# Dense stage of a three-stage kernel: six tiles of 512 tokens in place of eight of 384

## The chip, the cores and the metric

One core of a Trainium2 chip runs the whole program. The metric is device time in microseconds: 999.37 us for the kernel before, the median of three runs (998.09, 999.37 and 1006.32). The engines are TensorE (PE in the rows; its weight loads PEld), VectorE (DVE), ScalarE (ACT), GpSimd (POOL) and SyncE (SP), which only issues transfers here.

## What is computed

Three layers stand one behind the other on 3072 tokens of 512 features, all in fp32:

```python
# 1: attention with a decaying state, per batch (4) and head (8), 768 steps, head size 64
state = gamma * state + outer(k[t], v[t]);  y[t] = scale * (q[t] @ state)
# 2: mixture of experts: 8 experts, the best one by the gate for each token
e = argmax(x @ w_gate + modality_bias[modality_id])
out[mask] = gate_w[mask] * (relu(x[mask] @ w1[e]) @ w2[e])      # 512 -> 1024 -> 512
# 3: dense layer, 512 -> 2048 -> 512
h = x @ w_in
g = h * (1 / (1 + exp(-1.702 * h)))
out = g @ w_out
```

## The kernel before, in words

**Products of fp32 numbers.** Every factor is kept as two fp32r parts, a high one (`h`) and the rest (`l`), and a product is three matmuls: high by high, high by low, low by high. So a step's 4 blocks of 128 features make 12 matmuls in the dense stage's first product.

**Three stages.** Attention runs to about 140 us. From about 115 to 441.8 us the expert stage streams weights: a plan of *slots* (big ones of 256 tokens, B0 to B11, and two tiny ones, T0 and T1, of 32) is worked off by `run_slots`. The tokens of a slot are gathered from DRAM by index (`xg`, L650) and turned on TensorE (L673), the two products are L689 and L707, in tiny slots L738 to L778. The expert rows go to DRAM sorted by slot, with the token's number as one more column (513 columns, `DW`). The dense stage, 441.8 to 991 us, reads these sorted rows back, and scatters its results to the token's place.

**The stream of weights.** A piece is 512 KB, 128x1024. `load` (SyncE's queue, L572) fetches it into a ring of `nraw` = 4 raw buffers. `split` copies the high part on ScalarE (L593, `whi`), takes the rest on VectorE, or for some pieces on GpSimd (L595, `wlo`), and then asks `load` for the next piece: a raw buffer is free when both have read it. The engines work their instructions in program order, so a split that waits for its piece holds up what stands behind it on ScalarE and VectorE; in tiny slots that is the copy `htt` (L771), which the products of L778 read.

**The dense stage.** `T2` = 384 tokens are a tile, so there are 8 tiles of 3 rows (`NR`) of 128 tokens. A tile has 16 steps `f`, one for each 128 of the 2048 hidden features. `d1` does the first product of a step (12 matmuls into `psd`, L1104), the sigmoid on ScalarE (L1107, `sig`), `g` on VectorE (L1109), its high part `gh` on ScalarE (L1114) and the rest `gl` on VectorE (L1115). `d2` does the second product two steps later (`LAG`): for each row three matmuls of 512 columns into `psq` (L1125), one accumulator for each row, a single buffer of each. In the first steps `more_conv` puts the splitting of `w_out` between `g` and `gh`: lines 958 to 983 on ScalarE, VectorE and GpSimd. At the last step of a tile each row's accumulator is copied to `o` (VectorE L1129, ScalarE L1131) and scattered to DRAM by GpSimd (L1133).

**The rows of the next tile.** `yload` fetches a row of 128 tokens into `yg` on SyncE's queue in steps 5, 6 and 7; `turn` in steps 11, 12 and 13 copies the token numbers on GpSimd, turns the row on TensorE (four transposes, L1030) and splits it (ScalarE `yh` L1032, VectorE `yl` L1033). The rows of the first tile are fetched and turned inside the last slot of the expert stage, by a list `tail` of which each unit of work of that slot takes one entry. Behind the expert stage stands a branch (L1079) for slots beyond the plan, which is not taken here; each engine reads the condition and then goes on.

**Buffers.** `gt` (gh, gl) 3, `gg` (sig, g) 2, `yp` (yg) 3, `ot` (o) 3; in PSUM `psd` 3, the turned rows 2, each `psq` 1.

Of the kernel before, what the change touches and what calls it, by code (L numbers as in the profile page):

```python
# [8 lines left out]
F32 = mybir.dt.float32  # L9
# [3 lines left out]
AF = mybir.ActivationFunctionType  # L13
ALU = mybir.AluOpType
AX = mybir.AxisListType
PSUM = bass.MemoryType.PSUM
# [3 lines left out]
N, DM = B * S, H * D  # L20
E, FF = 8, 1024
DFF = 2048
C = 128
# [8 lines left out]
MAXB = 15  # L32
# [3 lines left out]
NB, NT_ = 12, 2  # L36
DW = DM + 1
RP1 = NP1 * BIG
T2 = 384
NF = DFF // C  # L40
AHEAD = 4

# [51 lines left out]
def tile_kernel(ctx, tc, qn, kv, mod, wg, mbias, w1, w2, w_in, w_out, c_qc, c_misc, out):  # L94
    nc = tc.nc
    V = nc.vector
    ctx.enter_context(tc.manual_schedule())
    pool = lambda st, name, bufs, side="left", space=None: st.enter_context(
        tc.tile_pool(name=name, bufs=bufs, side=side, reuse_waits="tile", **({"space": space} if space else {})))
# [10 lines left out]
    ident = M("id")  # L110
# [14 lines left out]
    mm = {}  # L125

    def open_sbuf(st_, nraw, nw):
        for nm, bufs in (("raw", nraw), ("w", nw), ("xg", 1), ("xt", 2), ("h", 3)):
            mm[nm] = pool(st_, "p_" + nm, bufs, "right")
        mm["nraw"], mm["nw"] = nraw, nw  # L130

    mo = ExitStack()
    open_sbuf(mo, 4, 6)


    pa = ExitStack()
# [234 lines left out]
    def T(nm, *sh):  # L371
        if nm not in tb:
            tb[nm] = ct(list(sh), "t_" + nm)
        return tb[nm]

    sc = T("sc", MAXB * E)
# [630 lines left out]

    NR = T2 // C
    NT2 = N // T2
    YG, YT, GT, PO = {}, {}, {}, {}  # L1010
# [1 line left out]
    pad("pad1", "left")  # L1012
    yt = [pool(ctx, "yt0", 1)]

    def yload(t, r, y=None):
        n = t * NR + r
        if y is None:
            y = yp.tile([C, DW], F32, name="yg", tag="yg")
        src, n0 = (ys0, 0) if n < RP1 // C else (ys1, RP1 // C)
        nc.sync.dma_start(y, src[(n - n0) * C:(n - n0 + 1) * C, :])  # L1020
        YG[t, r] = y

    def turn(t, r, ps):
        if r == 0:
            YT[t] = [yt[t % 2].tile([C, 4, T2], F32R, name=f"y{x}", tag=f"y{x}") for x in "hl"]
        y = YG.pop((t, r))
        n = t * NR + r
        nc.gpsimd.tensor_copy(idd[:, n:n + 1], y.bitcast(I32)[:, DM:DW])
        for k in range(4):
            nc.tensor.transpose(ps[:, k, :], y[:, k * C:(k + 1) * C], ident)  # L1030
        yh, yl = (x[:, :, r * C:(r + 1) * C] for x in YT[t])
        nc.scalar.copy(yh, ps)  # L1032
        V.tensor_tensor(out=yl, in0=ps, in1=yh.bitcast(F32), op=ALU.subtract)  # L1033

    def first_loads():
        y = mm["xg"].tile([C, 2, DW], F32, name="yg", tag="xg")
        for r in range(2):
            yload(0, r, y[:, r, :])

    def first_turn(r):  # L1040
        turn(0, r, mm["t"].tile([C, 4, C], F32, name="pyt", tag="pt"))
        if r == 1:
            yload(0, 2, mm["xg"].tile([C, DW], F32, name="yg", tag="xg"))

    cq = []

    def first_conv(stage):
        if stage == 0:
            cq.extend((Conv(NF + NE), Conv(NF + NE + 1)))
        else:  # L1050
            cq[0].A()
            cq[0].B()

    none = lambda: None
    tail = [first_loads, none, none, lambda: first_conv(0), lambda: first_turn(0), lambda: first_turn(1), none, none, lambda: first_turn(2), lambda: first_conv(1)]
    fin = table_final()
    for _ in range(FIN_SLOTS - 1):
        next(fin)
# [15 lines left out]
    mps.close()  # L1074
    mo.close()
    R_ = lambda name, bufs: pool(ctx, name, bufs, "right")
    gt, gg, yp, ot = R_("gt", 3), R_("gg", 2), R_("yp", 3), R_("ot", 3)
    ps_h = pool(ctx, "ps_h2", 3, "left", PSUM)
    with tc.If(tot > 0):  # L1079
        with ExitStack() as xs:  # L1080
# [12 lines left out]
    for f in range(NE, NF):  # L1093
        woh[f] = wo.tile([C, DM], F32R, name=f"woh{f}")
        wol[f] = wo.tile([C, DM], F32R, name=f"wol{f}")
    ps_o, ps_t = (pool(ctx, nm, b, "left", PSUM) for nm, b in (("ps_o2", 1), ("ps_t2", 2)))

    def d1(t, f, mid=None):
        yh, yl = YT[t]
        ps = ps_h.tile([C, T2], F32, name="psd", tag="psd")  # L1100
        m = 0
        for k in range(4):
            for a, b in ((wih, yh), (wih, yl), (wil, yh)):
                nc.tensor.matmul(ps, a[:, k, f * C:(f + 1) * C], b[:, k, :], start=(m == 0), stop=(m == 11), skip_group_check=True)  # L1104
                m += 1
        sig = gg.tile([C, T2], F32, name="sig", tag="sig")
        nc.scalar.activation(sig, ps, AF.Sigmoid, scale=1.702)  # L1107
        g = gg.tile([C, T2], F32, name="g", tag="g")
        V.tensor_tensor(out=g, in0=ps, in1=sig, op=ALU.mult)  # L1109
        if mid:  # L1110
            mid()
        gh = gt.tile([C, T2], F32R, name="gh", tag="gh")
        gl = gt.tile([C, T2], F32R, name="gl", tag="gl")
        nc.scalar.copy(gh, g)  # L1114
        V.tensor_tensor(out=gl, in0=g, in1=gh.bitcast(F32), op=ALU.subtract)  # L1115
        GT[t, f] = (gh, gl)

    def d2(t, fs):
        if fs[0] == 0:
            PO[t] = [ps_o.tile([C, DM], F32, name="psq", tag=f"psq{r}") for r in range(NR)]  # L1120
        for r in range(NR):
            for f in fs:
                gh, gl = GT[t, f]
                for m, (a, b) in enumerate(((gh, woh), (gh, wol), (gl, woh))):
                    nc.tensor.matmul(PO[t][r], a[:, r * C:(r + 1) * C], b[f], start=(f == 0 and m == 0), stop=(f == NF - 1 and m == 2), skip_group_check=True)  # L1125
            if f == NF - 1:
                o = ot.tile([C, DM], F32, name="o", tag="o")
                if r % 2:
                    V.tensor_copy(o, PO[t][r])  # L1129
                else:  # L1130
                    nc.scalar.copy(o, PO[t][r])  # L1131
                n = t * NR + r
                nc.gpsimd.indirect_dma_start(out=outv[n], out_offset=bass.IndirectOffsetOnAxis(ap=idd[:, n:n + 1], axis=0), in_=o, in_offset=None)  # L1133
        for f in fs:
            del GT[t, f]
        if f == NF - 1:
            del PO[t], YT[t]
# [3 lines left out]
    def more_conv(i):  # L1141
        if len(cq) < NF - NE:
            cq.append(Conv(NF + NE + len(cq)))
        at_ = lambda k: cq[k] if 0 <= k < NF - NE else None
        p0, p1, p2 = at_(i + 1), at_(i), at_(i - 1)
        for p, fs in ((p1, "C"), (p0, "A"), (p2, "E"), (p0, "B"), (p2, "F")):
            if p:
                getattr(p, fs)()

    for i, (t, f) in enumerate(seq):  # L1150
        d1(t, f, lambda: more_conv(i) if i <= NF - NE else None)
        if t + 1 < NT2:
            if f in (5, 6, 7):
                yload(t + 1, f - 5)
            elif f in (11, 12, 13):
                turn(t + 1, f - 11, ps_t.tile([C, 4, C], F32, name="pyt", tag="pyt"))
        if LAG <= i < len(seq):
            t, f = seq[i - LAG]
            d2(t, [f])
    d2(NT2 - 1, list(range(NF - LAG, NF)))  # L1160


# [32 lines left out]
```

## Time and profile before

| | us |
|---|---|
| median of three runs | 999.37 |
| the profiled execution | 1003.18 |
| its span, first to last instruction | 1001.5 |
| TensorE busy | 965.8 (96%) |
| VectorE busy | 504.3 (50%) |
| ScalarE busy | 410.3 (41%) |
| GpSimd busy | 177.7 (18%) |
| dense stage, first product L1104 to the last of L1125 | 441.79 to 991.1 |

The mean granted clock of TensorE is 0.988 of full speed. Busy shares are of the whole span and mix the stages; a matmul's record is longer than its share of a stream, since matmuls overlap, so paces are taken from start to start or from a chain of many.

### The profile page before, as it was taken

The numbers are of one execution on the slowest core, as the hardware profiler recorded it, in microseconds if no ns is written. First come the engines' busy times: TensorE is split into PE (matmuls) and PEld (weight loads), VectorE is DVE, ScalarE is ACT, GpSimd is POOL, SyncE is SP. The second block draws the span as 40 slices with busy tenths as digits, with TensorE's granted clock in tenths as the row PEclk, the third lists the DMA queues.
The fourth block names the chain that finished last, engine by engine and source line by source line (L and its number), as shares of the span: only waits on it lengthen the run. The fifth ranks groups of instructions, "written<-read, shape, count | busy, mean of one in ns | idle before, by whom it ended". The sixth has DMA issues, their size and how long they took to land.

```text
span 1001.5 us, 16732 instructions
## 1 busy us (share of the span) xinstructions
PE 965.8 (96%) x6610; PEld 857.7 (86%) x6610; DVE 504.3 (50%) x921; ACT 410.3 (41%) x728; POOL 177.7 (18%) x177
## 2 busy tenths in 40 slices
PE   8999879899999999999999999999999999999995
PEld 7878768799999997778999999999999999999994
DVE  3545559798888876549942322322323223223221
ACT  3423245477767765348742222222322222222221
POOL 2343334223333222003220010010000100100101
PEclk9999989999999999999999999999999999999998
DMA  8777668788788779834410100100001001000000
GB/s 287 222 210 204 113 227 213 251 267 275 285 277 278 262 249 341 304 116 170 136 43 1 32 32 1 32 32 12 26 27 32 32 1 32 32 1 1 32 1 31
DMA packets 43129, 128.18 MB, mean 128 GB/s; under 512 B 6977, under 2 KB 7361, under 8 KB 43041
## 3 DMA queue, kind: packets, MB, share of 16 engines
q1 hardware_dynamic: 34464, 107.96, 34.1%
q0 software_dynamic: 5120, 12.77, 3.6%
q10 hardware_dynamic: 3456, 6.29, 1.8%
q8 instruction: 53, 0.87, 0.4%
q14 instruction: 36, 0.29, 0.1%
HBM read 107.76 MB, written 19.24 MB: 127 GB/s over the span
## 4 chain that ended last, share of the span: by engine, by line
PE 54%; ACT 0%; DVE 0%; POOLq 0%; POOL 0%; issue 0%; ACTq 0%
PE psq L1125 27%; PE psd L1104 26%; PE pyt L1030 1%; ACT L1107 0%; POOLq L1191 0%; DVE ab L963 0%; DVE ab L965 0%; ACT o L1131 0%; ACT ab L958 0%; ACT ab L968 0%; ACT sig L1107 0%; DVE gl L1115 0%; DVE ab L964 0%; POOL out_dram L1133 0%; POOLq L1133 0%
## 5 line engine op out<-in xcount | busy, mean ns | idle before, releaser
L1109 DVE TENSOR_TENSOR g<-psd,sig 128x384 f32<-128x384 f32 x128 | 71.3, 557 | 278.4 <-ACT sig L1107 278.4
L1107 ACT ACTIVATE sig<-psd 128x384 f32<-128x384 f32 x128 | 63.0, 492 | 291.9 <-PE psd L1104 291.9
L1104 PE MATMUL psd<-yh,wih 128*128 128x384 f32 x512 | 172.8, 337 | 0.1
L1104 PE MATMUL psd<-yl,wih 128*128 128x384 f32 x512 | 172.7, 337 | 0.0
L1104 PE MATMUL psd<-yh,wil 128*128 128x384 f32 x512 | 172.6, 337 | 0.0
L1125 PE MATMUL psq<-woh,gh 128*128 128x512 f32 x384 | 153.9, 401 | 0.7 <-ACT gh L1114 0.7
L1125 PE MATMUL psq<-woh,gl 128*128 128x512 f32 x384 | 152.0, 396 | 1.1 <-DVE gl L1115 1.1
L1125 PE MATMUL psq<-wol,gh 128*128 128x512 f32 x384 | 151.7, 395 | 0.0
L595 DVE TENSOR_TENSOR wlo<-raw,whi 128x1024 fp32r<-128x1024 f32 x93 | 113.2, 1222 | 32.7 <-ACT whi L593 28.2
L593 ACT CAST whi<-raw 128x1024 fp32r<-128x1024 f32 x96 | 99.7, 1046 | 39.6 <-issue 17.8
L689 PE MATMUL psh<-xh,whi 128*128 128x256 f32 x384 | 109.7, 286 | 1.1 <-ACT xh L676 1.1
L689 PE MATMUL psh<-xl,whi 128*128 128x256 f32 x384 | 108.2, 282 | 0.1
L689 PE MATMUL psh<-xh,wlo 128*128 128x256 f32 x384 | 108.0, 281 | 0.0
L1133 POOL DMA_INDIRECT out_dram<-o,idd x24 | 23.3, 972 | 461.0 <-DVE o L1129 386.4
L1115 DVE TENSOR_TENSOR gl<-g,gh 128x384 fp32r<-128x384 f32 x128 | 71.5, 559 | 65.0 <-ACT gh L1114 65.0
L1104 PEld LDWEIGHTS psd<-yh,wih 128*128 128x128 f32 x512 | 96.3, 188 | 6.1 <-PEq L1079 0.5
L1104 PEld LDWEIGHTS psd<-yl,wih 128*128 128x128 f32 x512 | 96.3, 188 | 5.5
L1104 PEld LDWEIGHTS psd<-yh,wil 128*128 128x128 f32 x512 | 96.3, 188 | 0.0
L1114 ACT CAST gh<-g 128x384 fp32r<-128x384 f32 x128 | 65.7, 514 | 70.3 <-DVE g L1109 70.2
L1125 PEld LDWEIGHTS psq<-woh,gl 128*128 128x128 f32 x384 | 72.5, 189 | 18.6 <-DVE gl L1115 1.5
L1125 PEld LDWEIGHTS psq<-woh,gh 128*128 128x128 f32 x384 | 72.5, 189 | 12.4 <-ACT gh L1114 1.0
L1125 PEld LDWEIGHTS psq<-wol,gh 128*128 128x128 f32 x384 | 72.7, 189 | 11.5
(195 smaller groups left out, 1516.3 us busy)
## 6 DMA issues: line engine op xcount, KB each, us to landing
raw<-in_w_dram SPq DMA_DIRECT2D x96, 512.0 KB
qk<-in_qn_dram SPq DMA_DIRECT2D x23, 512.0 KB
r<-in_w_in_dram SPq DMA_DIRECT2D x16, 512.0 KB
r<-in_w_out_dram SPq DMA_DIRECT2D x16, 512.0 KB
ys<-yo SPq DMA_DIRECT2D x12, 513.0 KB
yg<-ys SPq DMA_DIRECT2D x24, 256.5 KB
v<-in_kv_dram SPq DMA_DIRECT2D x24, 256.0 KB
xd<-xr ACTq DMA_DIRECT2D x24, 256.0 KB
```

The costliest lines, as they stand in the source:

```text
L593: nc.scalar.copy(hi, raw)
L595: eng.tensor_tensor(out=lo, in0=raw, in1=hi.bitcast(F32), op=ALU.subtract)
L689: nc.tensor.matmul(ps[:, f, :], a[:, k, f * C:(f + 1) * C], b[:, k, :], start=(m == 0), stop=(m == 11), skip_group_check=True)
L1030: nc.tensor.transpose(ps[:, k, :], y[:, k * C:(k + 1) * C], ident)
L1104: nc.tensor.matmul(ps, a[:, k, f * C:(f + 1) * C], b[:, k, :], start=(m == 0), stop=(m == 11), skip_group_check=True)
L1107: nc.scalar.activation(sig, ps, AF.Sigmoid, scale=1.702)
L1109: V.tensor_tensor(out=g, in0=ps, in1=sig, op=ALU.mult)
L1114: nc.scalar.copy(gh, g)
L1115: V.tensor_tensor(out=gl, in0=g, in1=gh.bitcast(F32), op=ALU.subtract)
L1125: nc.tensor.matmul(PO[t][r], a[:, r * C:(r + 1) * C], b[f], start=(f == 0 and m == 0), stop=(f == NF - 1 and m == 2), skip_group_check=True)
L1133: nc.gpsimd.indirect_dma_start(out=outv[n], out_offset=bass.IndirectOffsetOnAxis(ap=idd[:, n:n + 1], axis=0), in_=o, in_offset=None)
```

## The change

The tile of the dense stage is made 512 tokens (6 tiles of 4 rows). To make room, the raw ring of the expert stage goes from 4 to 3 buffers, `yp` and `ot` from 3 to 2, `gg` from 2 to 1, and the turned rows in PSUM from 2 to 1. The sigmoid is written into `g`'s buffer and multiplied in place. The first tile's four rows are fetched on GpSimd's queue in two pairs, the second pair after the second turn, and the `tail` list turns a fourth row. A sigmoid of one column is issued beside the first pair. In the steady tiles rows 0 and 1 are fetched in steps 5 and 6, rows 2 and 3 in steps 11 and 12 behind the turns of rows 0 and 1, and turned in steps 13 and 14. The outputs of the last tile's rows 2 and 3 go through `yp`'s buffers.

```diff
-T2 = 384
+T2 = 512
...
-    open_sbuf(mo, 4, 6)
+    open_sbuf(mo, 3, 6)
...
-    def yload(t, r, y=None):
+    def yload(t, r, y=None, eng=nc.sync):
...
-        nc.sync.dma_start(y, src[(n - n0) * C:(n - n0 + 1) * C, :])
+        eng.dma_start(y, src[(n - n0) * C:(n - n0 + 1) * C, :])
...
-    def first_loads():
+    def first_loads(r0):
         y = mm["xg"].tile([C, 2, DW], F32, name="yg", tag="xg")
         for r in range(2):
-            yload(0, r, y[:, r, :])
+            yload(0, r0 + r, y[:, r, :], nc.gpsimd)
+        if r0 == 0:
+            nc.scalar.activation(T("sc", MAXB * E)[:, 0:1], ident[:, 0:1], AF.Sigmoid)
...
         if r == 1:
-            yload(0, 2, mm["xg"].tile([C, DW], F32, name="yg", tag="xg"))
+            first_loads(2)
...
-    tail = [first_loads, none, none, lambda: first_conv(0), lambda: first_turn(0), lambda: first_turn(1), none, none, lambda: first_turn(2), lambda: first_conv(1)]
+    tail = [lambda: first_loads(0), none, none, lambda: first_conv(0), lambda: first_turn(0), lambda: first_turn(1), none, lambda: first_turn(2), lambda: first_turn(3), lambda: first_conv(1)]
...
-    gt, gg, yp, ot = R_("gt", 3), R_("gg", 2), R_("yp", 3), R_("ot", 3)
+    gt, gg, yp, ot = R_("gt", 3), R_("gg", 1), R_("yp", 2), R_("ot", 2)
...
-    ps_o, ps_t = (pool(ctx, nm, b, "left", PSUM) for nm, b in (("ps_o2", 1), ("ps_t2", 2)))
+    ps_o, ps_t = (pool(ctx, nm, b, "left", PSUM) for nm, b in (("ps_o2", 1), ("ps_t2", 1)))
...
-        sig = gg.tile([C, T2], F32, name="sig", tag="sig")
-        nc.scalar.activation(sig, ps, AF.Sigmoid, scale=1.702)
         g = gg.tile([C, T2], F32, name="g", tag="g")
-        V.tensor_tensor(out=g, in0=ps, in1=sig, op=ALU.mult)
+        nc.scalar.activation(g, ps, AF.Sigmoid, scale=1.702)
+        V.tensor_tensor(out=g, in0=ps, in1=g, op=ALU.mult)
...
-                o = ot.tile([C, DM], F32, name="o", tag="o")
+                last = t == NT2 - 1 and r >= 2
+                o = yp.tile([C, DW], F32, name="yg", tag="yg")[:, 0:DM] if last else ot.tile([C, DM], F32, name="o", tag="o")
...
-            if f in (5, 6, 7):
+            if f in (5, 6):
                 yload(t + 1, f - 5)
-            elif f in (11, 12, 13):
+            if 11 <= f < 11 + NR:
                 turn(t + 1, f - 11, ps_t.tile([C, 4, C], F32, name="pyt", tag="pyt"))
+                if f < 13:
+                    yload(t + 1, f - 9)
```

## Rows read from the trace of the kernel before

**Rows 1.** Page, part 4: the chain that ended last, shares of the span by line.
```profile
PE psq L1125 27%; PE psd L1104 26%; PE pyt L1030 1%; ACT L1107 0%; POOLq L1191 0%; DVE ab L963 0%; DVE ab L965 0%; ACT o L1131 0%; ACT ab L958 0%; ACT ab L968 0%; ACT sig L1107 0%; DVE gl L1115 0%; DVE ab L964 0%; POOL out_dram L1133 0%; POOLq L1133 0%
```
**Rows 2.** Windows: stretch, length, busy of PE, PEld, DVE, ACT, POOL, PEclk, DMA, GB/s.
```profile
441.80:456.20 14.40, 12.60 (x57) 11.17 (x58) 8.04 (x13) 10.32 (x19) 4.07 (x3) 0.88 0.42 142
524.60:934.00 409.40, 409.40 (x2087) 370.67 (x2086) 122.06 (x216) 111.24 (x222) 19.54 (x33) 1.00 0.07 22
450.80:454.20 3.40, 3.39 (x9) 2.71 (x10) 2.79 (x5) 3.09 (x7) 1.29 (x1) 0.53 0.43 154
183.00:186.00 3.00, 0.33 (x1) 0.14 (x1) 2.57 (x11) 1.03 (x1) 0.00 (x0) 1.00 0.86 304
```
**Rows 3.** Chain in order of time: start, us, engine, tile, line, matmuls.
```profile
638.39 2.12 PE psd L1104 x12
640.51 2.10 PE psq L1125 x9
...
655.20 2.08 PE psd L1104 x12
```
**Rows 4.** Timeline, TensorE: start, us, engine, line, operation. Nine matmuls lie between these.
```profile
437.18 0.39 PE L707 MATMUL pso<-whi,hl 128*128 128x512 f32 x1
...
439.22 0.39 PE L707 MATMUL pso<-whi,hl 128*128 128x512 f32 x1
```
**Rows 5.** Timeline, the dense stage's first step; in brackets the idle before and its releaser.
```profile
445.15 1.28 ACT L1107 ACT_TABLE_LOAD   x1 [2.78 <-ACTq L1079]
...
450.81 0.67 PE L1125 MATMUL psq<-woh,gl 128*128 128x512 f32 x1 [1.07 <-DVE gl L1115]
```
**Rows 6.** Timeline, slot T0: SyncE's issues, ScalarE's splits, TensorE.
```profile
384.99 0.33 SPq L572 DMA_DIRECT2D raw<-in_w_dram  x1
387.33 8.42 SPq L572 DMA_DIRECT2D raw<-in_w_dram  x4
...
393.08 1.05 ACT L593 CAST whi<-raw 128x1024 fp32r<-128x1024 f32 x1 [2.11 <-DMA raw<-in_w_dram]
...
396.38 0.62 PE L778 MATMUL psq<-whi,htt 128*32 128x512 f32 x1
...
397.76 1.05 ACT L593 CAST whi<-raw 128x1024 fp32r<-128x1024 f32 x1 [0.72 <-DMA raw<-in_w_dram]
```
**Rows 7.** Timeline, slot T1: ScalarE's splits, TensorE.
```profile
422.44 1.05 ACT L593 CAST whi<-raw 128x1024 fp32r<-128x1024 f32 x1 [1.46 <-DVE wlo L595]
...
423.07 0.66 PE L1030 MATMUL pyt<-misc,yg 128*128 128x128 f32 x4 [1.33 <-DMA yg<-ys]
...
426.91 0.62 PE L778 MATMUL psq<-whi,htt 128*32 128x512 f32 x1
...
427.81 1.04 ACT L593 CAST whi<-raw 128x1024 fp32r<-128x1024 f32 x1 [0.63 <-DMA raw<-in_w_dram]
```
**Rows 8.** Timeline, first slots of the expert stage: GpSimd and TensorE.
```profile
170.80 2.40 POOL L595 TENSOR_TENSOR wlo<-raw,whi 128x1024 fp32r<-128x1024 f32 x1 [3.12 <-DVE t_cxS L365]
...
180.96 0.98 POOL L650 DMA_INDIRECT xg<-xd,ix  x1 [0.30 <-issue]
...
185.30 0.33 PE L673 MATMUL pxt<-misc,xg 128*128 128x128 f32 x1 [2.35 <-DMA xg<-xd,ix]
```
**Rows 9.** Timeline, one step of the dense stage with the splitting of w_out.
```profile
490.02 0.49 ACT L1107 ACTIVATE sig<-psd 128x384 f32<-128x384 f32 x1 [1.16 <-PE psd L1104]
...
494.47 0.55 DVE L1115 TENSOR_TENSOR gl<-g,gh 128x384 fp32r<-128x384 f32 x1
494.64 0.49 ACT L1107 ACTIVATE sig<-psd 128x384 f32<-128x384 f32 x1 [1.08 <-PE psd L1104]
```
**Rows 10.** Timeline, GpSimd at the end of a tile.
```profile
587.61 0.98 POOL L1133 DMA_INDIRECT out_dram<-o,idd  x1 [64.38 <-DVE o L1129]
...
588.90 0.96 POOL L1133 DMA_INDIRECT out_dram<-o,idd  x1 [0.30 <-issue]
```
**Rows 11.** Windows, the stretch behind that second scatter.
```profile
589.10:590.00 0.90, 0.90 (x5) 0.73 (x4) 0.54 (x1) 0.33 (x1) 0.76 (x1) 1.00 0.76 291
```

## The prediction

> **What bounds the kernel now.** I read the page first. Its chain of the work that ended last runs through TensorE, and half the span is two lines, the dense stage's second and first products (L1125, L1104) [rows 1]. Then the table of windows: in the dense stage's steady part TensorE is busy all of 409.40 us, VectorE 122 and ScalarE 111; in its first 14.40 us TensorE is idle for 1.8, and right behind that the granted clock is 0.53 over 3.4 us, the lower level (1.2 GHz) for nearly all of it; 3 us almost without matmuls at 183 did not lower it [rows 2]. So in the dense stage only fewer TensorE nanoseconds, or a new wait, move the end. Before 441.8 the expert stage is bound by TensorE too, but fed by a tight stream of weights.
>
> **Width of the first product.** A step of it is 12 matmuls in 2.08 to 2.12 us, 173.3 to 176.7 ns each (I use 175); a step of the second is 9 matmuls of 512 columns in 2.10 us, 233.3 ns (over many steps 232) [rows 3]. In the expert stage the same 512 columns go in (439.22 − 437.18)/9 = 226.7 ns [rows 4]. All are 0.44 to 0.46 ns per column, so the columns cost and not the instruction, and the columns stay the same. Before: 8 tiles x 16 steps x 12 = 1536 matmuls x 175 = 268.8 us. After: 6 x 16 x 12 = 1152, of 512 columns: at 226.7 ns 261.2 (−7.6), at 232.2 267.5 (−1.3), at 233.3 about 0. The second product has 1152 matmuls before and after (267.3 at 232), at 226.7 −6.1. Which pace the new step settles at no row shows. I take 229.5 for both, midway between two rows equally near: −4.4 and −2.9, **−7.3**; bounds −13.7 and 0.
>
> TensorE: Matmul & The Clock Gate in the Trainium skill (section "Wait — 56ns, not 53.3ns?") gives a stream of warm matmuls N/2.4 GHz plus about 2.5 ns each. By it 384 matmuls fewer would save 1.0 us, an estimate from that page, in place of the −7.3. The paces above are slower than it says.
>
> **Dense start.** The first step takes 441.8 to 456.2, 14.40 us [rows 2], where four first products and one second are 10.5. ScalarE loads the sigmoid's table at 445.15, having waited 2.78 us at the branch; the second product then waits 1.07 for `gl` [rows 5]. After, the table comes earlier and each first product lasts 2.75 us: 8.25 us of cover before the second product, and I count `gl` ready 8.0 after the start. All but the 1.8 us idle and 2.2 of lost clock go: **−4.0** (−4.2 to −2.5). If the table is late still, `gl` is next.
>
> **One raw weight buffer less, T0.** Pieces of weights go over SyncE's queue into the ring, ScalarE splits them in order (L593), VectorE follows (L595) and then copies `htt`, for which TensorE's L778 waits. With three buffers a piece is issued when the next one was. In slot T0 the piece of 384.99 then goes out at 387.33, and lands when its successor did: its split moves from 393.08 (already 2.11 late on its DMA) to 397.76, where the next one waited 0.72 on its own [rows 6]. That is 4.68 us; L778 at 396.38 moves with it. **+4.6** (0 to 5: nothing if the queue, having one transfer less in it, delivers that much sooner).
>
> **T1.** The same: the split of 422.44 moves to that of 427.81, less 1.4 for the two row loads that are no longer on the queue; L778 at 426.91 moves to about 430.5, and the 1.33 us that TensorE waits on `yg` at 423.07 goes [rows 7]. **+2.2** (0 to 4). In the big slots I charge nothing: a piece there is split 8 us after its issue, as the one above would have been, and one slot later still leaves it in time with a queue less full; without that cover each costs up to the 2.11 above.
>
> **Rows on GpSimd's queue.** Four row loads leave SyncE's queue, where they stood among the raw pieces, and stand on GpSimd's behind its own splits, 2.40 each [rows 8]; they are asked for four units of work ahead of their use: 0 (0 to +2.4). The table load beside them puts 1.28 on ScalarE [rows 5] in the last slot; nothing there is late by the rows I read: 0 (0 to +1.3).
>
> **Early stream.** On its queue GpSimd has the split at 170.80, 2.40 long, before the gather of 180.96, and TensorE waits 2.35 for `xg` at 185.30 [rows 8]. A ring of three puts the split about 1 us later. **+1.0** (0 to 2.5).
>
> **Clock.** Three new idles of TensorE (T0, T1, early). At 183 3 us made no drop, at 450 a shorter one did [rows 2]; a drop costs 3.4 us at half speed, 1.7. I take one: **+1.7** (0 to 3.4).
>
> **Single `g`.** In the first 15 steps the conversion of `w_out` sits between `g` and `gh`. From the sigmoid at 490.02 to the end of `gl`, 494.47 + 0.55, is 5.00 us, longer than a step of 4.2; it goes only because the next sigmoid, 494.64, starts before that end, in the second buffer [rows 9]. After, it may not: 5.00 + 0.10 (sigmoid) + 0.13 (`gl`) + 0.05 = 5.28 per step, against 24 x 0.2295 = 5.5 on TensorE. So it fits, but wears off the first steps' lag (about 4.8 us, from the 8.0 above) by only 0.2 a step, and where the rows turn (step 11), one PSUM buffer for the transposes makes TensorE wait for VectorE: **+2.7** once (0 to 4).
>
> **Tile boundaries.** Two output buffers: the third row's output waits for the first's scatter, the fourth's for the second's. A scatter occupies POOL 0.98, the next comes 1.29 later [rows 10], and the transfers burst behind the second (291 GB/s at 589.1 [rows 11]). The next tile wants the fourth row's accumulator 2 x 2.75 + 3 x 0.7 = 7.6 us after the old tile's end; its copy waits for the second scatter and that one's burst, and I count it free at 8.1: 0.5 x 5 boundaries = **+2.5** (0 to 8). The end itself, four rows instead of three, each 1.39 us of matmuls against 1.29 of scatter: **−0.5**. The transposes keep their number, four to a row in 24 rows: 0. Yp's two buffers are loaded again at steps 11 and 12, after the turn that frees them, and wanted two steps later, 11 us: 0.
>
> **Sum.** −7.3 − 4.0 + 4.6 + 2.2 + 1.0 + 1.7 + 2.7 + 2.5 − 0.5 = **+2.9**. The profiled execution took 1003.18 (span 1001.5), the median 999.37, 3.81 less; so 1006.1 in a profile and **1002** as a median.
>
> **Rivals.**
> A, *the faster pace*: all 512-wide matmuls settle at 226.7 ns. For: they have done so in the expert stage for 13 slots. Against: in the dense stage the same width has not. −13.7 in place of −7.3: 996.
> D, *the ring is deep enough*: the pieces land in time, no stall in T0, T1 or early, clock kept. For: fewer transfers share the queue. Against: the waits of 2.11 and 0.72 on DMAs [rows 6]. −8.5: 994. With A, 987.
> B, *no faster pace*: 232 to 233 ns stay. For: that is what this stage shows. +6.2 to +7.3: 1008.5.
> The Trainium skill's rule above is B's neighbour: 1.0 saved where B has 0 to 1.3.
> C, *the loop of the single `g` decides*, the slower side: the loop exceeds TensorE's step of 5.5. For: with 5.28 little is left, and GpSimd's or VectorE's conversion lengthening by 0.3 does it. Against: the row gives 5.28. At 6.0 it is 15 steps x 0.5 = 7.5, and 1.0 of lag that never wears off: +8.5, 1011.
> E, *the early table does nothing*: the load comes again after the branch. Then 1.3 of the start's gain is gone: 1003.6, within the forecast's range.
> The Trainium skill's ScalarE activation tables: per-element evaluation and per-set limits (section "Table sets in the compiler and the runtime") says that the compiler places the table loads per block, which speaks for E. Before, the only load besides the kernel's first stands behind the branch [rows 5]; that the sigmoid is first used there explains it as well.
>
> **How the numbers follow.** Forecast 0.40 (997 to 1007, E with it), A 0.15, D 0.12, A and D together 0.10, B 0.12, C 0.11. About 1% (10 us) is what a measurement of this kernel can tell from no change, so faster is below 989.4 and slower above 1009.4. Faster: 0.08 of A with D, 0.03 of A, 0.04 of D = 0.15. Slower: 0.08 of C, 0.05 of B, 0.05 of the forecast with its bounds at their ends = 0.18. Same 0.67. The range 990 to 1012 leaves out most of A with D, and the far ends of C and of the boundaries.
>
> **What would show it.** L1104's 12 matmuls in 2.75 us (2.72 A, 2.79 B). ScalarE's split in T0 and T1 starting with a wait on its DMA, L778 near 401 and 430; none of it in D. No table load behind L1079, and 0.53 gone from the granted clock at 451. VectorE's `gl` followed by the sigmoid in the first 15 steps, 5.3 us apart (6.0 in C). One wait at L1030 near step 11, and at each boundary half a microsecond at L1125's fourth row. I am wrong if the dense stage falls by over 12 us, or the stages before it grow by over 12.

## The result and the profile after

The changed kernel takes 1015.63 us (median of four runs, 1014.23 to 1019.27) against 1000.62 before: a ratio of 1.0145, interval 1.0117 to 1.0173. It is slower by 15 us, and outside the forecast range of 990 to 1012. Ratios, here and below, leave out the executions of a slower state that some of them fall into; the traces of two experiments, e1 and e7, are of such executions, and from these only idles and paces are read. The profiled execution took 1016.1 (span 1014.5), 13.0 of span more than before.

The span splits at the first matmul of the dense stage: 441.79 before, 449.32 after, so 7.5 of the 13 are lost ahead of it. With TensorE's instructions matched one to one, the changed kernel is 3.9 ahead just before T0's matmuls, 2.8 behind after them, 6.8 behind after T1's (1.4 regained between them at `yg`), and 7.5 at the dense stage, with one turn more. The 3.9 can't be put down to the change: a second trace of the changed kernel (e5) began its dense stage 6.2 us later than this one. From its first matmul to the end of the span the dense stage takes 559.7 before and 565.1 after, the other 5.4.

**Ahead of the dense stage.** Timeline of the changed kernel, slot T0 (the rows that answer to [rows 6]): SyncE's issues, ScalarE's split, VectorE's copy, TensorE.

```profile
383.66 15.91 SPq L572 DMA_DIRECT2D raw<-in_w_dram  x5
...
394.24 1.04 ACT L593 CAST whi<-raw 128x1024 fp32r<-128x1024 f32 x1 [3.51 <-DMA raw<-in_w_dram]
...
397.06 0.42 DVE L771 COPY htt<-ptt 128x256 f32<-128x256 f32 x1
...
397.53 1.06 PE L778 MATMUL psq<-whi,htt 128*32 128x512 f32 x1 [5.03 <-DVE htt L771]
```

A split waits 3.51 us for its piece, VectorE's `htt` stands behind it, and TensorE waits 5.03, where the matmuls of L778 waited for nothing in the kernel before. T1, timeline of the same kernel (against [rows 7]):

```profile
429.34 1.04 ACT L593 CAST whi<-raw 128x1024 fp32r<-128x1024 f32 x1 [2.90 <-DMA raw<-in_w_dram]
...
432.03 1.04 PE L778 MATMUL psq<-whi,htt 128*32 128x512 f32 x1 [3.67 <-DVE htt L771]
```

The records of the 16 matmuls of L778 in each slot are then 1.06 us long (they overlap), where the median was 0.59. The windows of the changed kernel say why (columns as in [rows 2]; the second is the start of the dense stage, the third the stretch behind the turn at 516, the last its steady part):

```profile
397.50:401.10 3.60, 3.57 (x16) 0.60 (x16) 1.71 (x2) 0.83 (x2) 1.07 (x2) 0.50 0.66 226
449.30:460.60 11.30, 11.28 (x49) 9.14 (x50) 5.72 (x9) 6.45 (x12) 2.60 (x2) 1.00 0.44 144
517.60:520.30 2.70, 2.70 (x8) 2.10 (x7) 2.63 (x4) 1.95 (x4) 1.06 (x2) 0.50 0.23 66
524.60:934.00 409.40, 406.74 (x1774) 325.98 (x1774) 119.86 (x176) 103.45 (x178) 26.31 (x40) 1.00 0.07 24
```

Behind each of the three idles of 5.03, 3.67 and 2.10 us TensorE ran at a granted clock of 0.50, the lower level, in this trace. Each of T0 and T1 costs 1.7 us more by it: 16 matmuls in 3.65 us in place of 1.97.

**The dense stage.** The start is as forecast: TensorE is busy 11.28 of 11.30 us, no table load stands behind the branch (it went to the last slot, timeline of ScalarE):

```profile
417.50 1.28 ACT L1040 ACT_TABLE_LOAD   x1
418.79 0.20 ACT L1040 ACTIVATE t_sc<-misc 128x1 f32<-128x1 f32 x1
```

The pace is not. Chain in order of time of the changed kernel, a stretch of tile 2 (answers to [rows 3]):

```profile
648.40 2.80 PE psd L1106 x12
651.20 2.79 PE psq L1126 x12
...
676.34 2.79 PE psd L1106 x12
```

Both products need 2.79 to 2.80 us for 12 matmuls, 233 ns each: five steps in 27.94. A step is 5.59 us here and 5.61 in the odd tiles, on average 5.60 for 512 tokens, 4.19 for 384 before; 96 steps are 537.5 and 128 were 536.1. Width alone gained nothing.

The chain of the same kernel at the end of a tile, and VectorE's and TensorE's timeline there:

```profile
642.56 4.02 DMA out_dram<-o,idd x2
...
646.70 0.70 DVE o L1131
...
647.44 0.96 PE psq L1126 x3
```

```profile
738.64 0.69 DVE L1131 COPY o<-psq 128x512 f32<-128x512 f32 x1 [4.04 <-DMA out_dram<-o,idd]
...
739.39 0.51 PE L1126 MATMUL psq<-woh,gh 128*128 128x512 f32 x1 [0.43 <-DVE o L1131]
```

VectorE has been idle for 4.04 us at this copy, which waits for the scatter that reads its buffer. That scatter was issued at 735.81, 2.83 us before the copy: 1.2 of the idle was the wait for its issue behind the first one. The step in which each of the five later tiles begins its second product is 0.3, 0.7, 0.7, 1.5 and 0.7 longer than the others: 3.9 us. Last, the turn of the second row in step 12 (timeline, TensorE and VectorE):

```profile
515.61 0.68 DVE L1033 TENSOR_TENSOR yl<-pyt,yh 128x512 fp32r<-128x512 f32 x1
...
516.35 0.66 PE L1030 MATMUL pyt<-misc,yg 128*128 128x128 f32 x4 [2.10 <-DVE yl L1033]
```

That step is 9.88 us, 3.84 over a step with a turn: 2.3 for the wait and 1.5 at the lower clock. The two can be told apart by e8 below, where the same wait of 2.10 was followed by no drop of the clock: from the transposes to the next first product it took 3.30 us there, and 4.84 here. Timeline of e8, and the window that answers to the third above:

```profile
515.53 0.66 PE L1030 MATMUL pyt<-misc,yg 128*128 128x128 f32 x4 [2.10 <-DVE yl L1033]
...
518.83 0.40 PE L1106 MATMUL psd<-yh,wih 128*128 128x512 f32 x1
```

```profile
516.60:519.30 2.70, 2.70 (x14) 2.16 (x12) 2.55 (x4) 2.12 (x5) 1.24 (x2) 1.00 0.26 77
```

Sum of the dense stage: start −3.9, pace +1.4, one turned row less −0.4, turn +3.9, ends of tiles +3.9, end +0.2: +5.1 of the 5.4.

### The profile page after: what moved, and what is told of

The parts are those of the page before. It is cut to its first block, busy times and chain, and to the rows that moved or that the text cites. A ratio compares the mean times of both kernels' runs of the same rounds, so it can differ in the third digit from the quotient of the medians.

```text
span 1014.5 us, 15787 instructions
## 1 busy us (share of the span) xinstructions
PE 968.6 (95%) x6226; PEld 801.4 (79%) x6226; DVE 498.4 (49%) x861; ACT 396.4 (39%) x661; POOL 181.4 (18%) x181
## 4 chain that ended last, share of the span: by engine, by line
PE 44%; DVE 4%; ACT 2%; DMA 2%; issue 2%; POOL 0%; POOLq 0%; DVEq 0%; ACTq 0%; SPq 0%
PE psd L1106 22%; PE psq L1126 21%; DMA out_dram<-o,idd 2%; DVE ab L963 1%; PE pyt L1030 1%; DVE gl L1116 1%; DVE wol L983 1%; DVE o L1131 1%; ACT ab L958 1%; ACT ab L968 1%; DVE ab L964 0%; ACT g L1109 0%; DMA r<-in_w_out_dram 0%; DVE g L1110 0%; ACT gh L1115 0%
## 5 line engine op out<-in xcount | busy, mean ns | idle before, releaser
L1110 DVE TENSOR_TENSOR g<-psd,g 128x512 f32<-128x512 f32 x96 | 66.4, 691 | 276.3 <-ACT g L1109 276.2
L1109 ACT ACTIVATE g<-psd 128x512 f32<-128x512 f32 x96 | 57.4, 598 | 303.3 <-PE psd L1106 279.2
L1126 PE MATMUL psq<-woh,gh 128*128 128x512 f32 x384 | 155.2, 404 | 2.7 <-DVE o L1131 1.3
L1126 PE MATMUL psq<-woh,gl 128*128 128x512 f32 x384 | 152.6, 397 | 0.0
L1126 PE MATMUL psq<-wol,gh 128*128 128x512 f32 x384 | 152.1, 396 | 0.0
L1106 PE MATMUL psd<-yh,wih 128*128 128x512 f32 x384 | 151.7, 395 | 0.4 <-PEq L1081 0.4
L1106 PE MATMUL psd<-yh,wil 128*128 128x512 f32 x384 | 151.5, 395 | 0.0
L1106 PE MATMUL psd<-yl,wih 128*128 128x512 f32 x384 | 151.2, 394 | 0.0
L1116 DVE TENSOR_TENSOR gl<-g,gh 128x512 fp32r<-128x512 f32 x96 | 66.5, 692 | 55.1 <-ACT gh L1115 55.0
L1126 PEld LDWEIGHTS psq<-woh,gh 128*128 128x128 f32 x384 | 72.4, 189 | 21.5 <-DVE o L1131 3.4
L1126 PEld LDWEIGHTS psq<-woh,gl 128*128 128x128 f32 x384 | 72.8, 190 | 17.8
L1106 PEld LDWEIGHTS psd<-yh,wih 128*128 128x128 f32 x384 | 71.9, 187 | 18.1 <-PEq L1081 0.8
L1106 PEld LDWEIGHTS psd<-yh,wil 128*128 128x128 f32 x384 | 71.9, 187 | 17.7
L1126 PEld LDWEIGHTS psq<-wol,gh 128*128 128x128 f32 x384 | 72.7, 189 | 16.6
L1115 ACT CAST gh<-g 128x512 fp32r<-128x512 f32 x96 | 59.6, 621 | 64.1 <-DVE g L1110 64.1
L969 POOL TENSOR_TENSOR sg<-ab,sg 128x512 f32<-128x512 f32 x32 | 50.7, 1584 | 187.9 <-ACT ab L968 164.7
```

What stands on the lines that cost most here:

```text
L969: nc.gpsimd.tensor_tensor(out=self.sg, in0=self.af, in1=self.sg, op=ALU.mult)
L1109: nc.scalar.activation(g, ps, AF.Sigmoid, scale=1.702)
L1110: V.tensor_tensor(out=g, in0=ps, in1=g, op=ALU.mult)
```

## The experiments

Each ran with the kernel before on its chip; ratios are against that one. Chips and runs differ by some us in the stages ahead of T0: the changed kernel's dense stage began at 449.32 in one trace and at 455.52 in another (e5). So single causes are read from the idle rows and from the length of the dense stage (to the end of the span), and totals from ratios of one chip. The dense stage of the changed kernel took 565.1 in one trace and 563.1 in the other, so a difference of 2 us between single traces shows nothing without the idle rows beside it.

**e5, the changed kernel again**, for e6 to e8.

> The changed kernel as it is, on the chip of the three kernels beside it, so that their times can be set against it. Every theory: 1.010 to 1.017 of the kernel before.

Ratio 1.0154 (1.0116 to 1.0192). The loss comes again; the dense stage is 563.1. The wait at the turn is there too, but the clock stays up behind it (timeline of e5, and a window in the columns of [rows 2]):

```profile
522.69 0.66 PE L1030 MATMUL pyt<-misc,yg 128*128 128x128 f32 x4 [2.26 <-DVE yl L1033]
```

```profile
523.00:526.00 3.00, 3.00 (x17) 2.46 (x15) 2.54 (x4) 2.88 (x6) 1.62 (x2) 1.00 0.31 119
```

This step took 8.51 us in place of 9.88. Of the four traces here with a wait of 2.1 to 2.4 us at the turn (the changed kernel, e5, e8, e14) only the first shows a drop behind it; the five with a longer one (2.6 to 4.0; e3, e6, e11, e12, e13) all show one.

### The ring

**e1, three raw buffers alone.**

```diff
# the kernel before
-    open_sbuf(mo, 4, 6)
+    open_sbuf(mo, 3, 6)
```

> The kernel before with one thing of the change alone: three raw weight buffers in place of four. Theory (the missing buffer delays the pieces of the slots T0 and T1): the matmuls of L778 move by about 5 us in T0 and 4 in T1, each followed by about 1.7 us at the lower clock; the dense stage starts 8 to 11 us later and the run is 8 to 11 us longer. Rival (the expert stage grew because the first rows moved to GpSimd's queue or because of the fourth turn): under 2 us.

Ratio 1.0098 (1.0062 to 1.0133), some 10 us. What TensorE waited for ahead of L778 in e1 (view of one line: the matmuls with their shortest, median and longest duration in ns; then us and times of the wait):

```profile
L778 PE MATMUL psq<-whi,htt x16: 1060/1061/1062, 415.0 to 454.2; 128*32 128x512 f32 x16
...
  DVE htt L771: 8.0, 2
```

The rival is out: nothing else of the change is in this kernel. The waits and the lower clock of T0 and T1 come with the ring alone, about two thirds of the loss.

**e2, the fourth buffer back.**

```diff
# the changed kernel
-    open_sbuf(mo, 3, 6)
+    open_sbuf(mo, 4, 6)
-    NE = 1
+    NE = 0
```

> The changed kernel with the fourth raw buffer back; the 4 KB for it come from converting no row block of w_out before the dense stage, where the changed kernel converts one. Theory: the idle of 5 us ahead of L778 in T0 and of 3.7 in T1 goes, the dense stage starts about 8 to 10 us earlier, the run is 8 to 10 us shorter than the changed kernel (about 1006). Rival: the ring costs nothing and the time stays at 1015.

Ratio 1.0055 (1.002 to 1.0089), against 1.0145 and 1.0154 for the changed kernel in other sessions: some 9 us shorter, in the range. The same view in e2:

```profile
L778 PE MATMUL psq<-whi,htt x16: 592/592/617, 401.8 to 432.6; 128*32 128x512 f32 x16
...
  DVE htt L771: 0.2, 1
```

The idle is gone and with it the lower clock. The price of my way to the 4 KB is in the trace too: the stage's first three first products and first second product take 16.62 us in place of 11.23, waiting for the first block of `w_out`. So the ring is worth more than this ratio shows; how much more isn't settled, since e1 puts the ring alone at 10.

### The pace

The paces of [rows 3] and [rows 4] were known to differ, and so were those of the second product's first step and its others (229 and 232 ns in even tiles of the kernel before). A matmul has a *stationary* operand, the weights that are loaded, and a *moving* one, whose columns stream through. In a listing of the SBUF (on-chip memory) addresses of both kernels the operands of the quick streams share something: the weights of the expert stage's slots, `hh`, and the first row block of `w_out` all begin 224 bytes above a multiple of 256; so do the stationary operands `w_in`, `gh` and `gl`. The turned rows (moving; in the changed kernel 0 in even tiles and 160 in odd ones, before 0 and 128) and the other blocks of `w_out` (128; before 96) do not.

**e3, other paddings.**

```diff
# the changed kernel; pad tiles are 32 bytes
-    pad("pad1", "left")
...
-    pad("pad2", "right")
+    pad("pad2", "right", 48)      # 192 bytes
```

> The changed kernel with other paddings alone: w_out's parts and the first of the two tiles of turned rows begin 224 bytes above a multiple of 256, as the weights of the expert stage and the first row block of w_out do; the second tile stays at 160. Theory (the pace of 227 ns of a 512-wide matmul hangs on where the moving operand lies): the second product falls from 233 to 234 ns to 228 or 229 in every tile, the first product from 233 to 228 in the even tiles and stays at 233 in the odd ones; 5 us from the second, 3 from the first, the run 6 to 9 us shorter than the changed kernel. Rival (the pace is set by something else, such as where a step's matmuls enter the pattern): every pace stays within 1 ns and the time within 2 us.

Ratio 1.0104 (1.0055 to 1.0153). The paces came as the theory said: first product 226.6 ns in even and 233.3 in odd tiles, second 226.7 and 228.5. The ratio fell by 0.4 to 0.5% only, less than its interval can tell; the wait at the turn grew from 2.1 to 3.7 us.

**e6, both tiles of turned rows at 224.**

```diff
# the changed kernel
-    pad("pad1", "left")
...
+    pad("pad2", "right", 48)
     yt.append(R_("yt1", 1))
-    pad("pad2", "right")
```

> The changed kernel with paddings alone: both tiles of turned rows and every part of w_out begin 224 bytes above a multiple of 256. Theory (address of the moving operand): first product 226.7 ns in even and odd tiles, second 226.7 to 229; a step 5.44 in place of 5.60, 96 steps, 14 to 16 us off the dense stage less up to 2 where the conversion loop takes over the first steps; run 12 to 15 us shorter than the changed kernel. Rival (odd tiles stay at 233, the earlier gain was something else in the even ones): 8 to 9.

Ratio 1.0088 (1.006 to 1.0117), 0.66% below e5 on the same chip, where 1.2 to 1.5% was expected. Chain in order of time of e6:

```profile
602.39 2.72 PE psq L1125 x12
605.11 2.73 PE psd L1105 x12
...
611.05 2.72 PE psd L1105 x12
```

226.7 ns for both products in every tile. Only addresses differ from the changed kernel, so addresses set the pace. Most of what is missing from the time went to the turn, where TensorE waits nearly twice as long as before (view of L1029, which is the changed kernel's L1030):

```profile
  DVE yl L1032: 4.0, 1
```

The conversion's steps take VectorE and ScalarE as long as before (5.3 us), TensorE's step is 5.44 now and can't make up the lag of the first steps. Behind the wait the clock drops, which costs 2.3 us (5.49 from the transposes to the next first product, 3.19 in the next tile); the ends of tiles are 1.2 longer. Dense stage 554.2 against 563.1.

**e7, the same in the kernel before.**

```diff
# the kernel before
-    pad("pad1", "left")
...
+    pad("pad2", "right", 40)      # 160 bytes
     yt.append(R_("yt1", 1))
-    pad("pad2", "right")
```

> The kernel before (tiles of 384, four raw buffers) with the same paddings alone. Theory: the second product falls from 232.5 to 227 or 229 ns (1152 matmuls, 4 to 6 us), the first from 174.9 to about 171 (1536 matmuls, 4 to 6 us): the dense stage 8 to 12 us shorter, ratio 0.988 to 0.992, so that it beats both kernels and tiles of 512 have no edge. Rival (the faster pace is there for 512 columns alone): the first product stays at 174 to 176, 4 to 6 us.

Ratio 1.0005 (0.9972 to 1.0038): a miss. Chain of e7:

```profile
646.72 2.08 PE psq L1124 x9
648.81 2.10 PE psd L1103 x12
```

175.7 ns for 384 columns, 231.2 for 512. The same addresses give 231 beside products of 384 and 227 beside products of 512. So the width does matter, but only together with the addresses: neither alone moves the time. At 384 columns equal addresses aren't the fastest either: in the kernel before, the first product took 176.7 ns in even tiles (moving operand at 0) and 173.6 in odd ones (128), the 2.12 and 2.08 us of [rows 3]. 5.44 us for 512 tokens are 4.08 for 384, 0.11 below e7's 4.19.

**e11, e13, e14, which addresses.** Paddings alone again, one execution each.

```diff
# e11: e6, and
-    pad("pad0", "left")
+    pad("pad0", "left", 56)       # w_in and the even tiles' rows 192 bytes on
# e13, e14: e6 with a pad ahead of each tile of turned rows and of w_out
```

> The changed kernel with all moving operands at 224, and then w_in's parts (the stationary operand of the first product), and with them the even tiles' turned rows, moved by 192 bytes: stationary 160; moving 160 in even tiles and 224 in odd ones. If the pace wants moving and stationary operand at one residue of 256: 226.7 in even tiles, 232 to 234 in odd. If it wants the moving one at 224, wherever the stationary is: 233 in even, 226.7 in odd. The second product has both at 224 and stays at 226.7.

> The changed kernel with the moving operand of the first product at 96 (even tiles) and 32 (odd tiles) modulo 256, that of the second at 160; stationary operands at 224. If equal residues modulo 256 are needed: 232 to 234 ns everywhere. If modulo 128: the even tiles' first product at 226.7, the rest at 232 to 234.

> The same with 192 (even tiles) and 64 (odd tiles), the second product at 192. If equal residues are needed: 232 to 234 everywhere. If nearness counts (192 is 32 below 224): even tiles and the second product between 227 and 231, odd tiles 233.

First product, ns for 512 columns by the residues modulo 256 of its two operands:

| stationary | moving | ns | run |
|---|---|---|---|
| 224 | 224 | 226.7 | e6 |
| 160 | 160 | 227.8 | e11, even tiles |
| 224 | 32 | 229.0 | e13, odd |
| 160 | 224 | 229.2 | e11, odd |
| 224 | 96 | 231.7 | e13, even |
| 224 | 0 | 232.6 | changed, even |
| 224 | 192 | 233.2 | e14, even |
| 224 | 160 | 233.3 | changed, odd |
| 224 | 64 | 233.5 | e14, odd |

One row from each end of the table, chains of e14 (odd tile) and of e11 (even tile):

```profile
585.09 2.81 PE psd L1107 x12
```

```profile
684.02 2.73 PE psd L1105 x12
```

In the first product equal residues are the fastest in both places of the stationary operand; equal modulo 128 (96) doesn't do, nor does nearness (192). But no simple rule of residues covers all rows: 32 is at 229.0, and the second product, 224 on both sides, took 226.7 to 227.2 ns in e11's odd tiles and 230.5 in its even ones, 226.7 in e3's even tiles and 228.5 in its odd ones, where only the operands of the first product beside it differ. That addresses set the pace is shown; the rule by which they do, and which part of the memory or of the engine it comes from, stays open.

### The waits of the dense stage

**e4, two PSUM buffers for the turned rows.**

```diff
# the changed kernel
-    ps_h = pool(ctx, "ps_h2", 3, "left", PSUM)
+    ps_h = pool(ctx, "ps_h2", 2, "left", PSUM)
...
-    ("ps_t2", 1)
+    ("ps_t2", 2)
```

> The changed kernel with two PSUM buffers for the turned rows, the bank taken from the first product's accumulators (two in place of three). Theory (the wait of 2.1 us at L1030 and the stretch at the lower clock behind it come from the single buffer meeting the late VectorE in the conversion steps): the wait at 514 goes and with it 1.3 us of lower clock, 3 to 4 us; unless two accumulators make TensorE wait at L1106 for the sigmoid and the product on VectorE, which reads the accumulator until about 1.5 us behind its last matmul and has a whole second product to do so. Net 2 to 4 us shorter than the changed kernel. Rival: the conversion loop of 5.3 us bounds the first steps, the wait moves to another instruction and the time stays.

Ratio 1.0104 (1.0068 to 1.014). No idle is left ahead of L1030 in its trace; the turning step is 6.04 us as in later tiles, and two accumulators cost nothing:

```profile
522.00:538.00 16.00, 16.00 (x75) 12.96 (x74) 13.68 (x21) 11.23 (x21) 4.87 (x6) 1.00 0.38 101
```

Dense stage 560.3 against 565.1 and 563.1 in the two traces of the changed kernel. The rival is out: the wait didn't move elsewhere. The clock stays at 1.00, but it did so in e5 with the wait, so e4 shows the price of the wait and not that of the clock.

**e8, outputs through the row buffers.**

```diff
# the changed kernel
-                last = t == NT2 - 1 and r >= 2
+                last = r >= 2
```

> The changed kernel, where the outputs of rows 2 and 3 of every tile go through the row buffers (yp), which the changed kernel does for the last tile alone. Theory (the wait at a tile's end is the third and fourth output waiting for the scatter of the first and second): the five idles of 0.3 to 1.4 us at L1126 go, 3 to 4 us. Rival (the fourth row's copy is late because ScalarE and VectorE have other work, or GpSimd's scatters are): they stay and the time within 1 us.

Ratio 1.0139 (1.0101 to 1.0176), against e5's 1.0154: the time alone doesn't tell them apart. The trace does. In the changed kernel TensorE sat idle ahead of L1126 (view of that line) until these:

```profile
  DVE o L1131: 1.3, 3
  ACT o L1133: 1.2, 1
```

In e8 neither row is left, the step at each of the five boundaries is 5.54 us, and the dense stage is 559.6 against 563.1.

**e12, without the early sigmoid.**

```diff
# the changed kernel
-        if r0 == 0:
-            nc.scalar.activation(T("sc", MAXB * E)[:, 0:1], ident[:, 0:1], AF.Sigmoid)
```

> The changed kernel without the sigmoid of one column in the last slot. Theory: a table load of 1.28 us stands behind the branch again, the first step's sigmoid is that much later, and since the step of 2.8 us has cover for about half a microsecond only, TensorE waits 0.5 to 1 us ahead of the first second product, and perhaps loses clock behind it (1.5). Rival (the wider step covers the load): no wait there.

The load is back behind the branch, and the stage's first three first products and first second product take 11.57 us in place of 11.23. Timeline of e12:

```profile
459.52 1.28 ACT L1107 ACT_TABLE_LOAD   x1 [3.00 <-ACTq L1079]
```

0.33 us, and no idle of TensorE that a row shows: the rival is right, and of the 3.9 that the start gained nearly all is the wider step's cover. But the delay is handed on to the turn, where TensorE waits 3.21 us in e12 against 2.10 and 2.26 in the two traces of the changed kernel.

### All together

**e9** takes e6, e4 and e8 together. **e10** adds e2's four buffers, and starts the conversion of the first block of `w_out` a step sooner:

```diff
# e9, and
             cq[0].B()
+            cq[0].C()
...
-        for p, fs in ((p1, "C"), (p0, "A"), (p2, "E"), (p0, "B"), (p2, "F")):
+        steps = ((p1, "E"), (p0, "A"), (p1, "F"), (p0, "B")) if i == 0 else (
+            (p1, "C"), (p0, "A"), (p2 if i > 1 else None, "E"), (p0, "B"), (p2 if i > 1 else None, "F"))
+        for p, fs in steps:
```

> The changed kernel with the paddings of all moving operands at 224, the outputs of rows 2 and 3 in the row buffers and two PSUM buffers for the turned rows; three raw buffers stay. Theory (the three causes in the dense stage are apart from each other and add up): dense stage 565 less 11 to 13 for the pace, 3.4 for the ends of tiles, 4 for the turn and the clock behind it, about 545 us; the run 990 to 996 against 1001 before, with the loss of T0 and T1 still in it. Rival (they share a cause, and the gain of one takes away the other's): 552 and 1002.

> The same with four raw buffers, the 4 KB from no early row block of w_out; the first block's conversion is brought one step forward, so that the second product doesn't wait for it as it did with four buffers before. Theory: T0 and T1 as in the kernel before, 7 to 9 us less than the run with three, 982 to 989. Rival: the wait on the first block stays, 3 to 5 us of it are given back.

On one chip, with 1007.86 for the kernel before: e9 1002.38, ratio 0.9944 (0.9912 to 0.9976); e10 995.86, ratio 0.9861 (0.9814 to 0.9908), faster than the kernel before, and by the ratios than the changed one. Dense stage 543.1 in e9: 559.7 less 16.6, and 22.0 below the first trace of the changed kernel. The three causes add up, and more: against e5 they gave 8.9, 3.5 and 2.8 one by one, 15.2, and 20.0 together, since with two buffers for the turn the faster pace no longer runs into it (from the third step on, every step without a turn is 5.44 us in e9). e10 is 6.5 below e9, just under the 7 to 9 expected, and the totals expected (990 to 996 and 982 to 989) had reckoned with 1001 for the kernel before. The idle ahead of L778, e9 and then e10:

```profile
  DVE htt L771: 9.5, 2
```

```profile
  DVE htt L771: 0.7, 1
```

e10's dense stage is 545.8, 2.7 longer than e9's, nearly what the rival had: the first block is still late, by 0.81 for its high part and 1.31 for the low one (timeline of e10):

```profile
464.42 0.51 PE L1126 MATMUL psq<-woh,gh 128*128 128x512 f32 x1 [0.81 <-ACT woh L980]
...
466.24 0.50 PE L1126 MATMUL psq<-wol,gh 128*128 128x512 f32 x1 [1.31 <-DVE wol L983]
```

## Why the prediction was wrong

- **Width of the first product: the step that failed.** −7.3 stood for the pace of both products at that width, and it was +1.4. I had the paces of both stages, 226.7 and 232, called the rows equally near and took the middle. They were not: the dense stage's own row was the nearer, and nothing in the change touched what made the other fast. That was rival B (0.12), 1008.5, which by itself would have stayed inside the range. The runs put the addresses of the operands in its place: at equal residues the term is what rival A said (e6: 5.44 a step, 96 steps 522.2, −13.9 against 536.1), in this kernel's layout it is nothing. A difference of pace between two stages with the same instruction was a question to be asked of the layout, not a range to be halved; [rows 3] had a smaller one inside the dense stage, 2.12 and 2.08 us for the same 12 matmuls, which I averaged.
- **The rule weighed there.** The Trainium skill's TensorE: Matmul & The Clock Gate (section "Wait — 56ns, not 53.3ns?") gives 215.7 ns from start to start for warm matmuls of 512 columns; the fastest stream here is 226.7. The 1.0 us that I had estimated from that page for 384 matmuls fewer was nearer than my −7.3, though nothing was saved (+1.4).
- **Dense start, −4.0: right** (−3.9), but by the width, not by the early table (e12, 0.33 here and about 1 at the turn). Rival E didn't happen: the load stays where its first use is. That the compiler places the table loads per block, which the Trainium skill's ScalarE activation tables: per-element evaluation and per-set limits (section "Table sets in the compiler and the runtime") says, made no second load behind the branch here.
- **Raw ring: the mechanism right, the size short.** T0's idle 5.03 against 4.6. T1's idle of 3.67 less the 1.4 gained at `yg` is 2.3 against 2.2 (my own terms, the split's 5.37 later less 1.4 and 1.33, come to 2.6). Rival D is out; its −8.5 had left out the early 1.0 that it names. What I left short is the clock.
- **Clock, +1.7: mis-sized.** I took one drop for three new idles; there were three in the profiled execution: 1.7 in T0, 1.7 in T1, 1.5 at the turn, 4.9 in all. The early idle that I had counted isn't among them; the one at the turn, which I had left out of the clock, is. [rows 2] held both cases, a drop and none, and I counted one in three. In T0 and T1 every trace of the changed kernel and of its variants with three raw buffers shows the drop; at the turn it came in one trace of four: the same wait of 2.1 to 2.4 us had none behind it in e5, e8 and e14.
- **Early stream, +1.0: not settled.** In the two traces the changed kernel lost 0.4 between 167 and 185 us, and the runs differ there by more.
- **Single `g`, +2.7: right**, 2.3 without the clock (2.5 in e5). The loop is 5.3, as worked out, and fits; the wait comes once, at the turn. Rival C didn't happen.
- **Tile boundaries, +2.5: 3.9.** The mechanism and its times came: counted from the start of the old tile's last second product (the prediction says its end), the fourth row's accumulator was wanted at 7.7 and free at 8.2. Four boundaries cost 0.3 to 0.7. The one near 831 us cost 1.5: there the first scatter kept its buffer for 4.3 us from its issue, at the other four for 2.8 to 2.9; why stays open. **The end, −0.5: +0.2**; nothing here shows why the gain of four rows didn't come.

The terms that failed: pace 8.7, clock 3.2, boundaries 1.4, end 0.7: 14.0 on top of +2.9. The profile showed 13.0, since the stages ahead of T0 happened to be 3.9 shorter; the other terms nearly cancel. The sign that I had named for being wrong, a change of over 12 us in the dense stage or ahead of it, didn't come: both grew, by 5.4 and 7.5.

## What to carry to other kernels

When one instruction runs at two paces in two stages, find the difference before you put either into a sum; here it was the operands' addresses, and paddings of 192 bytes and less were worth 9 us of the dense stage, but only at the width that could use it. A buffer that is given up in one stage to widen another is paid in the stage where transfers are tight, and the idles of 5.0 and 3.7 us there were paid twice, the second time by the clock. An idle of 2.1 us can go either way, so it is read from more than one trace. Waits that hide each other (the pace and the turn) show their gain only when both are removed.

## What the runs showed of the hardware that I had not expected

- The pace of a stream of 512-wide fp32r matmuls hangs on where its two operands lie: for the first product 226.7 and 227.8 ns at equal residues modulo 256, 229.0 to 233.5 at others, with paddings alone changed. It hangs on the matmuls beside it too: at equal residues the second product took 226.7 to 230.5 (e3, e11).
- At those addresses the 512-wide second product still takes 231.2 ns when it alternates with 384-wide matmuls (e7).
- An indirect scatter of 128 rows kept its source buffer for 2.8 to 2.9 us from its issue in eight of the changed kernel's ten cases, for 3.6 and 4.3 at one boundary. That is long behind the 0.96 us for which GpSimd is busy with it.
- The same wait of TensorE, 2.1 to 2.4 us ahead of the same transposes, was followed by a granted clock of 0.50 in one trace and of 1.00 in three.
